# A gate product in seven block products instead of eight, in three units of a two-layer convolution and SwiGLU kernel

## The chip, the cores and the metric

The kernel runs on one core of one Trainium2 chip. The metric is the device time of one execution in microseconds, the median of several runs. The engines of the core are named as in the profile: PE (TensorE matmul), PEld (its weight loads), DVE (VectorE), ACT (ScalarE), POOL (GpSimd) and SP (SyncE, which here only issues DMAs).

## The reference

Two layers, each with a long convolution (A) and a SwiGLU feed-forward part (B), on 2048 tokens of 512 features in bf16. The feed-forward part has 1792 hidden features.

```python
def _B_ref(x, w_gate, w_up, w_down):
    g = _silu(x @ w_gate)
    u = x @ w_up
    return (g * u) @ w_down

x = A_q
x = x + _A_ref(_layernorm(x), A_k, A_v, A_shift_k, A_ssm_k, A_ssm_D)
x = x + _B_ref(_layernorm(x), B_w_gate, B_w_up, B_w_down)
x = x + _A_ref(_layernorm(x), A_k, A_v, A_shift_k, A_ssm_k, A_ssm_D)
x = x + _B_ref(_layernorm(x), B_w_gate, B_w_up, B_w_down)
return x
```

A multiplies its normalised input by a convolution of k and v over the whole sequence, which doesn't depend on x. The change touches only B.

## The kernel before

The sequence is cut into four chunks of 512 tokens, and each chunk into two halves of 256. A unit (l, c, h) is the feed-forward part of layer l for half h of chunk c, so there are 16 units. The last four are those of chunk 3: (0,3,0), (0,3,1), (1,3,0) and (1,3,1). Between a unit of layer 0 and the unit of layer 1 of the same half stand the down product's adds, two layer norms (bn_stats and bn_aggr on DVE, the power for rstd on POOL, L939) with the multiplication by the convolution's result between them, and transposing DMAs on SP, which turn z into zT, the operand of the next gate and up products. While one half goes through that chain, PE works on the other half.

A unit's 14 tiles of 128 hidden features come in groups of 4, 4, 4 and 2 (`GROUPS`). For each group `ffn` computes a gate half and an up half and multiplies them. Group 0 of the first three of the last units is done row-wise (`by_rows`). In the others, feature tiles are the stationary operand and 256 tokens the moving one: for each pair of feature tiles 8 matmuls of 256 columns into one PSUM buffer (ring `pf`, 4 buffers), then one ACT evacuation of 512 elements, a silu for the gate (L1321) and a copy for the up half (L1325). The product of the two is a DVE instruction (L1330).

Two parts are already computed with seven block products instead of eight. `seven` (L1130) does it for the down product in the units that `STRASSEN` names, with sums of weights made once (`weight_sums`) and sums of the activations (tile `cb`, L1139 to L1143), and `add_seven` adds the results. `up_seven` (L1210) does it for the up product in the groups that `UP7` names, groups 1 and 2 of the last four units. It views a group's operands as 2 x 2 blocks: contraction halves by odd and even feature tiles for the weights, contraction halves by the two token rows for zT. `up_sums` makes five sums of weight blocks once for a group (L1196, kept in ring `s8`), `z_sums` five sums of token blocks once for a unit (three instructions, L1204 to L1208). The seven products are then matmuls of 128 columns, 28 for a group (7 products, 2 pairs of tiles, 2 contraction blocks), into four PSUM buffers. ACT copies these to the tile m7 (L1236: three of 512 elements and one of 256), and four DVE instructions add and subtract them into the up tile (L1240 to L1245).

The program is a list of operations, each with an engine, what it reads and what it writes. `ORDER` is a table with one entry for each operation in the sequence in which the code creates them: the entry is the operation's place in the order of issue. Every engine takes its operations in the order of these places. Buffers of a ring are handed out in that order too, so an operation may also wait until a buffer comes free. `mode` answers "A" where its last argument is true and "D" where it is not, because `SUPER` is empty.

Of the kernel before, what the change touches and what calls it, by code (L numbers as in the profile page):

```python
# [9 lines left out]
P = 128  # L10
# [23 lines left out]
UP7 = {(0,3,0): (1, 2), (0,3,1): (1, 2), (1,3,0): (1, 2), (1,3,1): (1, 2)}  # L34
# [99 lines left out]
]  # L134
R = 4
BN_SLOTS = 6
# [228 lines left out]
def kernel(  # L365
# [14 lines left out]
    nc = tc.nc  # L380
# [7 lines left out]
    W = HP * P  # L388
# [1284 lines left out]
```

## Time and profile before

| | us |
|---|---|
| median of three runs | 337.94 (337.67 to 338.55) |
| the profiled execution, whole | 337.59 |
| its span, first to last instruction | 335.6 |

The span is what the views of the profile show; 2.0 us of the profiled execution lie around it. In a row that groups instructions stand: the line, the engine, the operation, what it writes and reads, the shapes and the count, then busy us and mean ns of one, then the engine's idle time before them and what ended it. A row of the chain has its start, its length, the engine and line. A row of the timeline has start, length, engine and line; instructions that follow each other on one line are merged (x4). Instructions of one engine overlap a little, so the step from one start to the next tells more of the rate than the length of one.

### The profile page before, as it was taken

To read this page: it belongs to the slowest core of one execution; us is meant where nothing else is said; L and a number is where in the kernel's file an instruction comes from. 1 tells how busy PE (TensorE), PEld (TensorE's weight loads), DVE (VectorE), ACT (ScalarE), POOL (GpSimd) and SP (SyncE) were. 2 spreads that over 40 slices of the span, in tenths; PEclk is the share of its full clock that TensorE was granted. 3 is DMA by queue.
4 is the path that set the end of the run, shared out by engine and by line. 5 is a ranking of instruction groups with operands and counts; after the bars stand their busy time and mean duration, and the time that the engine had idled before them with its cause. 6 is when DMAs were issued, how large, how long until landed. Compare 5 with 4: busy or idle time off the path is not lost.

```text
span 335.6 us, 6388 instructions
## 1 busy us (share of the span) xinstructions
PE 331.0 (99%) x2342; PEld 212.1 (63%) x2342; DVE 314.1 (94%) x601; ACT 267.1 (80%) x532; POOL 39.7 (12%) x54
## 2 busy tenths in 40 slices
PE   9999999999999999999999999999999999999996
PEld 7666864745445564654544564674747887978994
DVE  8899999999999999999999999999988789999495
ACT  7889999999988675799899765967787647867473
POOL 4000110032020010311101101151000000000000
PEclk9999999999999999999999999999999999999999
DMA  7999503367744488930744586727323210202201
GB/s 289 323 297 364 74 16 80 63 117 151 157 94 84 92 164 167 197 72 5 152 80 89 115 165 154 130 57 143 79 47 80 58 38 1 64 20 51 60 2 63
DMA packets 77449, 37.37 MB, mean 111 GB/s; under 512 B 67685, under 2 KB 73706, under 8 KB 77418
## 3 DMA queue, kind: packets, MB, share of 16 engines
q1 hardware_dynamic: 75632, 30.61, 39.0%
q0 software_dynamic: 1632, 6.29, 10.6%
q8 instruction: 18, 0.29, 0.4%
q14 instruction: 13, 0.11, 0.1%
q10 hardware_dynamic: 154, 0.07, 0.1%
HBM read 12.33 MB, written 2.10 MB: 43 GB/s over the span
## 4 chain that ended last, share of the span: by engine, by line
PE 94%; DVE 2%; DMA 1%; ACT 1%; POOL 0%; issue 0%; DVEq 0%; POOLq 0%
PE pf L437 51%; PE pd L1350 17%; PE ps L1160 10%; PE ps L437 7%; PE pf L1234 4%; PE ps L585 2%; DMA zT<-z 1%; PE wm L1639 1%; PE ps L918 1%; PE pt L604 1%; POOL rstd L939 0%; ACT kc L731 0%; DVE bst L953 0%; DVE t L783 0%; ACT sg L1260 0%
## 5 line engine op out<-in xcount | busy, mean ns | idle before, releaser
L437 PEld LDWEIGHTS <-zT 128*128 128x128 bf16 x496 | 48.2, 98 | 54.7 <-DMA zT<-z 0.5
L437 PE MATMUL pf<-wg_sb,zT 128*128 128x512 bf16 x248 | 61.5, 379 | 0.0
L437 PE MATMUL pf<-wu_sb,zT 128*128 128x512 bf16 x248 | 61.0, 379 | 0.0
L437 PE MATMUL pf<-zT,wg_sb 128*128 128x256 bf16 x400 | 50.4, 273 | 0.0
L437 PEld LDWEIGHTS <-wg_sb 128*128 128x128 bf16 x400 | 38.7, 98 | 7.6 <-issue 0.3
L1260 ACT ACTIVATE sg<-pf 128x512 bf16<-128x512 f32 x62 | 36.7, 607 | 8.2 <-PE pf L437 7.6
L1261 ACT CAST hr<-pf 128x512 bf16<-128x512 f32 x62 | 36.0, 592 | 8.3 <-PE pf L437 6.4
L1321 ACT ACTIVATE sg<-pf 128x512 bf16<-128x512 f32 x50 | 30.0, 610 | 14.9 <-PE pf L437 12.0
L779 DVE TENSOR_TENSOR t<-X,G 128x4096 bf16<-128x4096 bf16 x18 | 40.9, 2282 | 0.0
L1350 PE MATMUL pd<-wd_sb,sg 128*128 128x512 bf16 x160 | 38.6, 379 | 0.0
L939 POOL TENSOR_TENSOR rstd<-mv,nhalf 128x2 f32<-128x2 f32 x23 | 20.6, 900 | 138.6 <-DVE mv L954 138.6
L437 PE MATMUL pf<-zT,wu_sb 128*128 128x256 bf16 x272 | 34.4, 273 | 0.0
L953 DVE BATCH_NORM_STATS2 bst<-xc 128x6 f32<-128x512 bf16 x46 | 29.9, 683 | 0.4
L437 PEld LDWEIGHTS <-wu_sb 128*128 128x128 bf16 x272 | 26.6, 98 | 5.2
L1350 PEld LDWEIGHTS <-sg 128*128 128x128 bf16 x160 | 15.6, 98 | 17.8 <-DMA sg<-hr 0.3
L1350 PE MATMUL pd<-wd_sb,ht 128*128 128x512 bf16 (+1 forms) x110 | 25.5, 367 | 0.0
L1160 PEld LDWEIGHTS <-cb 128*128 128x128 bf16 x230 | 22.2, 98 | 4.5 <-DVE cb L1139 0.5
L1325 ACT CAST ht<-pf 128x512 bf16<-128x512 f32 x34 | 19.9, 598 | 3.5 <-PE pf L437 3.4
L546 ACT ACTIVATE X<-ps 128x512 bf16<-128x512 f32 x32 | 19.1, 610 | 3.5 <-PE ps L437 1.8
L1172 ACT CAST mt<-ps 128x512 bf16<-128x512 f32 (+1 forms) x28 | 14.5, 539 | 7.8 <-PE ps L1160 7.4
L1236 ACT CAST m<-pf 128x512 bf16<-128x512 f32 (+1 forms) x32 | 16.0, 541 | 3.6 <-PE pf L1234 3.3
L1330 DVE TENSOR_TENSOR ht<-ht,sg 128x1024 bf16<-128x1024 bf16 (+1 forms) x33 | 17.8, 554 | 1.1 <-ACT sg L1321 0.6
(157 smaller groups left out, 598.2 us busy)
## 6 DMA issues: line engine op xcount, KB each, us to landing
Z<-t POOLq DMA_DIRECT2D x6, 1024.0 KB, 8.3
hn<-in_A_ssm_k_dram SPq DMA_DIRECT2D x4, 512.0 KB, 4.9
vt<-in_A_v_dram SPq DMA_DIRECT2D x4, 512.0 KB, 5.3
xc<-in_A_q_dram SPq DMA_DIRECT2D x4, 512.0 KB, 6.1
out_dram<-xc SPq DMA_DIRECT2D x15, 128.0 KB, 1.9
wg_sb<-in_B_w_gate_dram SPq DMA_DIRECT2D x1, 1792.0 KB
wu_sb<-in_B_w_up_dram SPq DMA_DIRECT2D x1, 1792.0 KB, 7.8
wd_sb<-in_B_w_down_dram SPq DMA_DIRECT2D x1, 1280.0 KB, 12.0
```

The source lines that it names most:

```text
L437: nc.tensor.matmul(o, lhsT=lhsT, rhs=rhs, start=(n == 0), stop=(n == len(terms) - 1))
L546: add("ACT", act(D), lambda: nc.scalar.activation(out=view(), in_=ps.t[:], func=ACT.Copy, scale=scale), r=[ps], w=[(buf, keys)], conv=conv)
L779: dve(8 * D, lambda t=t, part=part: nc.vector.tensor_mul(out=t.t[:], in0=x.t[:, :, part:part + 1, :].to_broadcast((P, R, 2, D)), in1=g.t[: ...
L939: add("POOL", cost, lambda: nc.gpsimd.tensor_tensor(out=rstd.t[:], in0=var(), in1=nhalf.t[:].to_broadcast((P, n)), op=ALU.pow), r=reads + ...
L953: add("DVE", 0.6, lambda st=st, i=i: nc.vector.bn_stats(out=st.t[:, 0:6], in_=xs[c].t[:, i, :]), r=[(xs[c], (i,))], w=[st])
L1160: nc.tensor.matmul(bank.t[:, half_ * C:(half_ + 1) * C], lhsT=lhsT(i), rhs=rhs(i), start=(first and i == 0 and half_ == 0), stop=(last and ...
L1260: add("ACT", act(D), lambda ps=ps, dst=dst, o=o, which=which: nc.scalar.activation(out=rows(dst, o), in_=ps.t[:], func=ACT.Silu) if which ...
L1261: out=rows(dst, o), in_=ps.t[:], func=ACT.Silu) if which == "g" else nc.scalar.copy(out=rows(dst, o), in_=ps.t[:]),
L1321: add("ACT", act(D), lambda ps=ps, o=o, sg=sg: nc.scalar.activation(out=sg.t[:, o:o + 2, :], in_=ps.t[:], func=ACT.Silu), r=[ps], w=[(sg, ...
L1325: add("ACT", act(D), lambda ps=ps, o=o, ht=ht: nc.scalar.copy(out=ht.t[:, o:o + 2, :], in_=ps.t[:]), r=[ps], w=[(ht, (o // 2,))], due=(uni ...
L1330: dve(n * W, lambda sg=sg, ht=ht: nc.vector.tensor_mul(out=ht.t[:], in0=ht.t[:], in1=sg.t[:]), [sg], [ht], due=(unit, k / pairs, 0.0, "h"))
L1350: nc.tensor.matmul((pds[o] if not cs.start else pds[HP]).t[:, cs], lhsT=ht.tiles(q, o), rhs=wt["d"].t[:, ft, cs], start=(ft == std0 and no ...
```

## The change

The gate half of group 1 is computed with seven block products too, in units (0,3,0), (0,3,1) and (1,3,0). In each of them two standard products (16 matmuls of 256 columns) and their two silu evacuations from PSUM go. In their place come four operations on PE with 28 matmuls of 128 columns, four ACT copies to a tile m7, four DVE instructions that put the block sums together in the gate tile, and one ACT silu over the whole gate tile (1024 elements, in SBUF, in place), which waits for the last of the four. Five sums of gate weight blocks are made once, in another buffer of ring `s8`, and kept until the last of the three units has used them. The sums of token blocks are the ones that the up product uses. `up_sums` and `up_seven` take the weight's name; the calls of `up_sums` and `z_sums` move from `up_seven` to the place before the group's products in the list of operations.

`ORDER` is replaced as a whole: 1881 entries instead of 1849 (3 x 9 operations more, and 5 weight sums). Units keep their sequence. Of the table only the line with the places of the five gate weight sums is shown: they are operations 1462 to 1466, counted from 0, and stand as 1373, 1374, 1408, 1321, 1358.

```diff
-UP7 = {(0,3,0): (1, 2), (0,3,1): (1, 2), (1,3,0): (1, 2), (1,3,1): (1, 2)}
+UP7 = {(0,3,0): (1, 2), (0,3,1): (1, 2), (1,3,0): (1, 2), (1,3,1): (1, 2), "any": (1, 2)}
+GATE7 = {(0,3,0): (1,), (0,3,1): (1,), (1,3,0): (1,), "any": (1, 2)}
...
 ORDER = [
...
+    1518, 1535, 1533, 1546, 1550, 1373, 1374, 1408, 1321, 1358, 1417, 1406, 1390, 1062, 962, 1367, 972, 1369, 1407, 1410, 1411, 1412, 1428,
...
-    def up_sums(gi, kw):
+    def up_sums(which, gi, kw):
...
-    def up_seven(unit, zT, ht, fts, gi, at):
+    def up_seven(unit, zT, ht, fts, gi, at, which="u", before=()):
...
-        if gi not in wsum:
-            up_sums(gi, kw)
-        if unit not in zsum:
-            z_sums(unit, zT, kw)
-        w7, z7 = wsum[gi], zsum[unit]
+        w7, z7 = wsum[which, gi], zsum[unit]
...
-                seven_up = gi in UP7.get(unit, ())
+                kw = dict(due=(unit, k / pairs, 0.0, "h"))
+                sevens_at = {}
+                for which, table in (("g", GATE7), ("u", UP7)):
+                    s7 = sevens_at[which] = mode(which, unit + (gi,), gi in table.get(unit, ())) if c == 3 and gi in table.get("any", ()) else "D"
+                    if s7 in "AB":
+                        if (which, gi) not in wsum:
+                            up_sums(which, gi, kw)
+                        if unit not in zsum:
+                            z_sums(unit, zT, kw)
                 for o in range(0, n, 2):
-                    for which in ("g",) if seven_up else ("g", "u"):
+                    for which in "gu":
+                        if sevens_at[which] == "A":
+                            continue
...
-                if seven_up:
-                    up_seven(unit, zT, ht, fts, gi, k / pairs)
+                for which, dst in (("g", sg), ("u", ht)):
+                    if sevens_at[which] == "D":
+                        continue
+                    plan.cond = ((which,) + unit + (gi,), "A") if sevens_at[which] == "B" else None
+                    dst.steps = (W, P)
+                    up_seven(unit, zT, dst, fts, gi, k / pairs, which)
+                    if which == "g":
+                        add("ACT", 1.1, lambda sg=sg: nc.scalar.activation(out=sg.t[:], in_=sg.t[:], func=ACT.Silu), w=[sg],
+                            due=(unit, k / pairs, 1.0, "a"))
+                    plan.cond = None
```

More of the change, by code (lines that the diff above doesn't have):

```diff
@@ L33 @@
 STRASSEN={(0,2,1):4,(1,2,0):4,(1,2,1):4,(0,3,0):4,(0,3,1):4,(1,3,0):4,(1,3,1):2}
-UP7 = {(0,3,0): (1, 2), (0,3,1): (1, 2), (1,3,0): (1, 2), (1,3,1): (1, 2)}
+UP7 = {(0,3,0): (1, 2), (0,3,1): (1, 2), (1,3,0): (1, 2), (1,3,1): (1, 2), "any": (1, 2)}
+GATE7 = {(0,3,0): (1,), (0,3,1): (1,), (1,3,0): (1,), "any": (1, 2)}
+MODE0 = lambda g: int(g[4] in (UP7 if g[0] == "u" else GATE7).get(g[1:4], ()))
 I_RING = lambda k: "pf" if k == 3 else "pc"
@@ L1186 @@
     wsum, zsum = {}, {}
-    def up_sums(gi, kw):
+    def up_sums(which, gi, kw):
         fts = range(sum(GROUPS[:gi]), sum(GROUPS[:gi + 1]))
         m = len(fts) // 2
-        t = wsum[gi] = new("s8", "wu", [P, 5, KD // 2, m, P], parts=5)
-        part = lambda k, f: wt["u"].t[:].rearrange("p k (t f) -> p k t f", f=P)[:, 2 * k:2 * k + 2, fts[0] + f:fts[-1] + 1:2]
+        t = wsum[which, gi] = new("s8", "w" + which, [P, 5, KD // 2, m, P], parts=5)
+        part = lambda k, f: wt[which].t[:].rearrange("p k (t f) -> p k t f", f=P)[:, 2 * k:2 * k + 2, fts[0] + f:fts[-1] + 1:2]
         for n, (a, b, op) in enumerate((((0, 0), (1, 1), ALU.add), ((0, 1), (1, 1), ALU.add), ((0, 0), (1, 0), ALU.add),
@@ L1196, in up_sums @@
             dve(2 * m * P, lambda n=n, a=a, b=b, op=op: nc.vector.tensor_tensor(out=t.t[:, n], in0=part(*a), in1=part(*b), op=op),
-                [wt["u"]], [(t, (n,))], **kw)
+                [wt[which]], [(t, (n,))], **kw)
     def z_sums(unit, zT, kw):
@@ L1208, in z_sums @@
         dve(K2 * P, lambda: nc.vector.tensor_add(out=t.t[:, 0], in0=at(0, [[W, K2]]), in1=at(K2 * W + P, [[W, K2]])), [zT], [(t, (0,))], **kw)
-    def up_seven(unit, zT, ht, fts, gi, at):
+    def up_seven(unit, zT, ht, fts, gi, at, which="u", before=()):
         m, K2 = len(fts) // 2, KD // 2
         kw = dict(due=(unit, at, 0.0, "h"))
-        if gi not in wsum:
-            up_sums(gi, kw)
-        if unit not in zsum:
-            z_sums(unit, zT, kw)
-        w7, z7 = wsum[gi], zsum[unit]
+        w7, z7 = wsum[which, gi], zsum[unit]
         mt = new("s8", "m7", [P, 4, 2, m, P], parts=4)
-        raw = lambda k, f, i: (lambda kk: wt["u"].t[:, k * K2 + kk, (fts[0] + 2 * i + f) * P:(fts[0] + 2 * i + f + 1) * P])
+        raw = lambda k, f, i: (lambda kk: wt[which].t[:, k * K2 + kk, (fts[0] + 2 * i + f) * P:(fts[0] + 2 * i + f + 1) * P])
         summed = lambda n, i: (lambda kk: w7.t[:, n, kk, i])
@@ L1224, in up_seven @@
         for n, (rd, terms) in enumerate((
-                ([wt["u"], (z7, (2,))], ((lambda i: raw(0, 0, i), both(3)), (lambda i: raw(1, 1, i), both(4)))),
+                ([wt[which], (z7, (2,))], ((lambda i: raw(0, 0, i), both(3)), (lambda i: raw(1, 1, i), both(4)))),
                 ([w7, zT], ((lambda i: summed(2, i), tok(1, 1)), (lambda i: summed(1, i), tok(0, 0)))),
@@ L1308, in ffn @@
                 ht.tiles, ht.steps = (lambda q, o, ht=ht: ht.t[:, q, o * P:(o + 1) * P]), (W, P)
-                seven_up = gi in UP7.get(unit, ())
+                kw = dict(due=(unit, k / pairs, 0.0, "h"))
[7 more added lines that the diff above has]
+                            z_sums(unit, zT, kw)
                 for o in range(0, n, 2):
-                    for which in ("g",) if seven_up else ("g", "u"):
+                    for which in "gu":
+                        if sevens_at[which] == "A":
+                            continue
+                        plan.cond = ((which,) + unit + (gi,), "D") if sevens_at[which] == "B" else None
                         ps = new("pf", "pf", [P, D], F32)
@@ L1326, in ffn @@
                                 r=[ps], w=[(ht, (o // 2,))], due=(unit, k / pairs, 1.5, "a"))
+                        plan.cond = None
                     k += 1
-                if seven_up:
-                    up_seven(unit, zT, ht, fts, gi, k / pairs)
+                for which, dst in (("g", sg), ("u", ht)):
[7 more added lines that the diff above has]
+                            due=(unit, k / pairs, 1.0, "a"))
+                    plan.cond = None
                 dve(n * W, lambda sg=sg, ht=ht: nc.vector.tensor_mul(out=ht.t[:], in0=ht.t[:], in1=sg.t[:]), [sg], [ht],
```

151 rows, old and new, of the table ORDER are left out of this document.

## The prediction, made before the changed kernel was run

> **What bounds the kernel now.** I read the page's busy times first, and then asked whether the busy engine is also the one that sets the end.
>
> ```profile
> span 335.6 us, 6388 instructions
> PE 331.0 (99%) x2342; PEld 212.1 (63%) x2342; DVE 314.1 (94%) x601; ACT 267.1 (80%) x532; POOL 39.7 (12%) x54
> PE 94%; DVE 2%; DMA 1%; ACT 1%; POOL 0%; issue 0%; DVEq 0%; POOLq 0%
> ```
>
> PE is busy 331.0 of 335.6 us, and the chain of work that ended last (third line) runs through PE for 94% of the span. So a column taken from PE shortens the kernel, as long as nothing makes PE wait. DVE stands second with 314.1 us, so the next question is where DVE has room. I cut the program into stretches: the middle, the way into the last four units, and one stretch for about each of those.
>
> ```profile
> 88.00:216.00 128.00, 127.98 (x694) 67.53 (x691) 126.97 (x183) 103.26 (x209) 14.88 (x15) 1.00 0.58 117
> 216.00:256.00 40.00, 39.53 (x264) 25.19 (x262) 37.58 (x89) 30.20 (x56) 7.71 (x8) 1.00 0.43 83
> 256.00:281.00 25.00, 25.00 (x246) 20.90 (x244) 20.70 (x59) 15.37 (x31) 0.38 (x1) 1.00 0.21 43
> 281.00:298.00 17.00, 17.00 (x170) 14.01 (x168) 16.14 (x45) 12.72 (x24) 1.40 (x2) 1.00 0.18 41
> 298.00:315.00 17.00, 17.00 (x169) 14.01 (x167) 15.34 (x42) 9.38 (x19) 1.39 (x2) 1.00 0.23 56
> 315.00:333.00 18.00, 17.38 (x180) 15.04 (x177) 13.31 (x33) 13.00 (x27) 0.00 (x0) 1.00 0.06 18
> ```
>
> The columns after the length are busy us of PE, weight loads, DVE, ACT and POOL, then granted clock, DMA share and GB/s. From 88 to 216 us PE and DVE are both full: DVE idles 1.03 us in 128. In the last units PE stays full and DVE has room: 2.42, 4.30, 0.86, 1.66 and 4.69 us in the five later rows. ACT has at least 4 us in each. The clock is 1.00 throughout. Last, what does PE wait for? These are the rows of its weight loads after the first 40 us (us in total, times, longest), and the two of the matmuls themselves.
>
> ```profile
> PEld L437 <- DMA zT<-z: 0.5, 1, 0.5
> PEld L1160 <- DVE ht L1330: 0.5, 1, 0.5
> PEld L1160 <- DVE cb L1139: 0.5, 1, 0.5
> PEld L1350 <- DMA sg<-hr: 0.3, 1, 0.3
> PEld L1160 <- DVE cb L1143: 0.2, 1, 0.2
> PEld L1350 <- DVE ht L1330: 0.2, 1, 0.2
> PE ps L1160 <- DVE ht L1330: 0.3, 1, 0.3
> PE ps L1160 <- DVE cb L1139: 0.2, 1, 0.2
> ```
>
> All waits of the weight loads come to 2.2 us, 1.4 of it on DVE, and only 0.5 shows through as matmuls that waited. That is all that a better order can win after the start. The new table keeps every other operation on its engine and the units in their sequence; SP's transposes and POOL's operations are shuffled with the rest, none moves to another queue.
>
> **The products themselves.** In each of three units the standard gate product of one group, 16 matmuls of 256 columns, gives way to 28 of 128 columns (seven products, two pairs of feature tiles, two contraction blocks). The chain shows both shapes in unbroken runs:
>
> ```profile
> 305.90 3.49 PE pf L437 x32
> 320.79 1.56 PE pf L1234 x28
> ```
>
> 3.49 / 32 = 0.109 us for one of 256 columns, 1.56 / 28 = 0.0557 us for one of 128. So 16 x 0.109 = 1.745 us become 1.56: 0.185 us less in a unit, and 0.56 us in three. The second row is just such a group in this kernel, so I take it as it stands. The columns alone (512 fewer of 4096 in a unit) would save 12.5%, of which 10.6% is left.
>
> A rule speaks against this. The rows that group all 128-column products by operands are these:
>
> ```profile
> L1234 PE MATMUL pf<-zs,wu 128*128 128x128 bf16 x96 | 7.5, 219 | 0.0
> L1234 PE MATMUL pf<-zs,wu_sb 128*128 128x128 bf16 x64 | 4.9, 219 | 0.0
> L1234 PE MATMUL pf<-zT,wu 128*128 128x128 bf16 x64 | 4.7, 219 | 0.0
> ```
>
> They are busy 17.1 us for 224, which is 0.076 us each, because the modelled tail of each short run is counted along. The Trainium skill (TensorE: Matmul & The Clock Gate, Back-to-back issue gap) says that in a real stream of weight load and matmul pairs a matmul of 128 columns takes some 81 ns, not the isolated 56. By it a unit's 28 would take 2.27 us, and the edit would lose 0.5 us a unit. The run of 28 in 1.56 us disagrees with that rule, and it decides for the sum.
>
> **What DVE and ACT get.** The steps:
>
> ```profile
> 268.26 0.42 DVE L1242 TENSOR_TENSOR m<-m 128x512 bf16<-128x512 bf16 x1
> 268.60 0.42 DVE L1245 TENSOR_TENSOR ht<-m 128x512 bf16<-128x512 bf16 x1
> L1236 ACT CAST m<-pf 128x512 bf16<-128x512 f32 x24 | 13.5, 594 | 2.7 <-PE pf L1234 2.4
> L1236 ACT CAST m<-pf 128x256 bf16<-128x256 f32 x8 | 3.1, 385 | 0.9 <-PE pf L1234 0.9
> L1321 ACT ACTIVATE sg<-pf 128x512 bf16<-128x512 f32 x50 | 30.0, 610 | 14.9 <-PE pf L437 12.0 <-DMA sg<-hr 2.2 <-ACT z L1004 0.3
> L614 ACT COPY hs<-pt 128x1024 bf16<-128x1024 bf16 x2 | 2.0, 1020 | 0.0
> L718 ACT COPY hr<-hn 128x512 bf16<-128x512 bf16 x8 | 5.4, 685 | 0.0
> L614 ACT COPY hs<-pt 128x512 bf16<-128x512 bf16 x2 | 1.1, 576 | 0.0
> ```
>
> A sum of 512 elements steps DVE by 268.60 - 268.26 = 0.34 us. Five weight sums once are 1.7 us, four block sums in each of three units are 12 x 0.34 = 4.1 us: 5.8 us on DVE. The token sums existed before and are only created earlier. ACT loses two silus from PSUM (1.22 us) and gains three evacuations of 512, one of 256 and a silu over 1024 elements in SBUF, which the trace doesn't have: a copy of 1024 from PSUM took 1.02, and SBUF instead of PSUM cost 0.685 - 0.576 = 0.11 at 512, so 1.13 as an estimate from these rows. That is 1.78 + 0.385 + 1.13 - 1.22 = 2.1 us a unit, 6.2 in all, under ACT's room of at least 4 us a row.
>
> DVE's 5.8 us meet 2.42 + 4.30 + 0.86 + 1.66 = 9.24 us of room from 216 to 315. They cost nothing if the order spreads them so; without that cover each us in front of a down product is a us of PE. The new table's five entries for the weight sums are 1373, 1374, 1408, 1321 and 1358, which is the approach to unit (0,3,0) and not the full stretch before 216. Nothing is added there, so I count no cost for them, and at worst their 1.7 us.
>
> **The added wait.** The one silu now waits for the last block sum on DVE, and behind it on ACT stand evacuations that free PE's four PSUM buffers. In unit (1,3,0) the silu's place is 1751, DVE's product with the up half 1752, and PE's first matmuls that read the product come next in PE's queue. What covers the silu's 1.13 us is only how far ACT and DVE run ahead of PE there, so this edge is thin; it hangs on the same DVE queue as the next one, and I price them together.
>
> **The order's other thin edge.** The first product of the last unit (1,3,1) needs zT, which comes from the down product of (0,3,1) through adds, two layer norms and transposing DMAs. In the kernel before:
>
> ```profile
> 296.65 0.93 PE L1160 MATMUL ps<-wsa,cb 128*128 128x256 bf16 x7
> 297.42 0.61 PE L1234 MATMUL pf<-zs,wu_sb 128*128 128x128 bf16 x8
> 307.74 2.50 SPq L1061 DMA_TRANSPOSE zT<-z  x2
> zT<-z SPq DMA_TRANSPOSE x4, 2.4
> 313.82 1.04 PE L437 MATMUL pf<-zT,wg_sb 128*128 128x256 bf16 x8
> ```
>
> PE is done with (0,3,1) at 297.42 and reads the new zT at 313.82, 16.4 us later. The second transpose is issued 1.25 us (half of 2.50) after 307.74 and lands 2.4 us on, at 311.4: a chain of 14.0 us with 2.4 to spare. In the old table 7 matmuls of (1,3,0)'s down product stand behind that first read (entries above 1742), in the new one 25 (entries above 1764). So 18 x 0.109 = 1.96 us of work no longer lies in between, and 0.19 of the gate product is gone: 16.4 - 2.15 = 14.25 us for a chain of 14.0. The spare time falls from 2.4 to about 0.2 us. On DVE that chain now has (1,3,0)'s four gate sums among its entries, 1.36 us, while other sums have moved behind. A wait here costs between nothing (the sums fill gaps in which rstd and DMAs run) and 1.36 - 0.2 = 1.2 us; I take nothing: from the last add of (0,3,1) to the second z the old table has six sums and two products of 1024 elements beside the norms, the new one eight sums and one product, which is about the same work.
>
> **The sum.** PE -0.56, waits unchanged: 337.59 (the profiled execution, 335.6 of span and 2.0 around it) becomes 337.03. The median of the three runs, 337.94, is 0.35 above it, so what should be measured beside it is 337.94 - 0.56 = **337.4**. A measurement of this kernel can tell about 0.3%, 1.01 us, from no change: from 336.93 to 338.95 counts as the same.
>
> **The rivals.**
>
> 1. *The new order also removes waits.* The 1.4 us on DVE and 0.5 on zT go, of which 0.5 at least was PE's own. It would come to -0.56 - 0.5 to -0.56 - 1.4, that is 336.9 to 336.0; I put it at 336.4. For it: the waits are few and in places that the new table shuffles. Against: DVE is full up to 216, the waits on cb and ht stand at its end, and the new table takes no DVE work out ahead of it.
>
> 2. *The last zT comes late.* Its place is the first read by (1,3,1), decided by whether the chain exceeds 14.25 us; from 1.57 us of wait on the result is slower by over 0.3%. Price: 1.2 us of gate sums, and a rstd on POOL that DVE holds up.
>
> ```profile
> L939 POOL TENSOR_TENSOR rstd<-mv,nhalf x23: 686/710/2572, 29.9 to 306.0; 128x2 f32<-128x2 f32 x23
> ```
>
> Its median is 710 ns and its longest 2572, 1.86 us more, which gives 337.94 - 0.56 + 1.2 + 1.86 = 340.4; with 1.6 us of wait it would be 339.0. Against it: from 281 to 315 the four spans on POOL took 1.40 + 1.39 us, 0.70 each, beside a DVE that was busy all along. The Trainium skill (SBUF — State Buffer, Who interferes with whom) says that a DVE instruction with two SBUF inputs holds off a GpSimd instruction that reads SBUF for its whole length; the longest rstd agrees, and every added sum is of that kind.
>
> 3. *Products of 128 columns don't hold their pace.* At the grouped rows' 0.076 us 28 take 2.13 us, 0.39 more than before in each unit: 337.94 + 1.2 = 339.1. By the page named above it would be 339.5. The unbroken run of 28 speaks against it.
>
> **How the numbers follow.** Forecast 0.46, rival 1 0.31, rival 2 0.18, rival 3 0.05. Rival 1 lies below 336.93: faster 0.31. Same is 0.46. Rivals 2 and 3 give slower 0.23. Forecast and rival 1 hold 77%, and the forecast's own range is 336.9 to 338.6 (its wait of up to 1.2 us). For 8 in 10 the range takes in rival 1 to 336.2 and the lower part of rivals 2 and 3 to 339.4.
>
> **What would show it.** Right: 28 added products at 0.056 us, PE's busy time lower by about half a us, DVE up by some 6 us with its busy share in 256 to 315 above nine tenths, and no new row on zT or ht among PE's waits in the last units. A wait of over 1.5 us at the first read of (1,3,1), or one on ht of (1,3,0), means rival 2. A run of 28 that takes over 2 us means rival 3. If the old waits on cb and ht are gone and no others came, it is rival 1. I am wrong in kind if PE's waits lie before 216, where the change adds no work and only the order differs.

## The result and the profile after

The changed kernel took 340.64 us (median of five runs, 340.31 to 341.93), the kernel before 337.67 beside it (337.13 to 338.55): a ratio of 1.0092, 95% interval 1.0078 to 1.0107. The forecast was 337.4 with a range up to 339.4, so the kernel is 3.2 us slower than forecast and outside the range. The profiled execution took 340.31 us. Its page, span and busy times first, then the chain that ended last by engine and by line:

```profile
span 338.5 us, 6471 instructions
PE 331.5 (98%) x2378; PEld 210.6 (62%) x2378; DVE 318.2 (94%) x618; ACT 272.9 (81%) x541; POOL 45.1 (13%) x54
PE 38%; DVE 33%; ACT 11%; DMA 7%; issue 6%; POOL 3%; SPq 0%; POOLq 0%; DVEq 0%; ACTq 0%
PE pf L441 16%; PE ps L1164 8%; DMA Z<-t 6%; PE pf L1234 5%; PE ps L441 4%; DVE bst L957 3%; POOL rstd L943 3%; DVE t L783 3%; DVE m L671 3%; DVE t L787 3%; DVE hr L1267 3%; PE ps L589 2%; ACT z L1008 2%; DVE n L1057 2%; ACT hr L1261 1%
```

The busy times hardly tell the two kernels apart: PE has half a microsecond more, probably because the modelled tail of the matmul ahead of a gap counts as busy and there are more gaps (at 84 us a matmul starts 0.86 us later than the usual step, and 0.70 of it shows as idle). The chain tells them apart. It ran through PE for 94% of the span and now does for 38%; DVE, ACT, the transfer Z<-t and the rstd on POOL have come into it. The same stretches as before, and one ahead of them (columns as in the prediction):

```profile
40.00:88.00 48.00, 47.30 (x276) 26.83 (x275) 46.12 (x71) 47.89 (x95) 10.06 (x8) 1.00 0.46 81
88.00:216.00 128.00, 126.89 (x680) 65.79 (x678) 124.79 (x178) 100.49 (x202) 16.67 (x15) 1.00 0.60 117
216.00:256.00 40.00, 39.30 (x266) 25.28 (x265) 38.13 (x89) 30.64 (x59) 8.55 (x7) 1.00 0.41 77
256.00:281.00 25.00, 25.00 (x233) 19.07 (x232) 24.03 (x71) 17.57 (x33) 0.69 (x1) 1.00 0.36 70
281.00:298.00 17.00, 17.00 (x183) 14.15 (x182) 15.21 (x40) 14.05 (x27) 1.41 (x2) 1.00 0.12 25
298.00:315.00 17.00, 17.00 (x183) 14.14 (x182) 16.58 (x47) 12.82 (x25) 1.38 (x2) 1.00 0.25 56
```

From 256 to 315 us, where the change is, PE is full as before: 25.00, 17.00 and 17.00. From 88 to 216, where nothing was added, PE idles 1.11 us instead of 0.02 and DVE 3.21 instead of 1.03. To see where the time goes I added up the columns that PE has worked off in both kernels and compared the times at which they reach the same amount. The changed kernel is level until 76 us, 0.6 us late at 88, 1.1 at 108, 1.7 at 132, 2.2 at 148, 2.3 at 212, 2.6 at 232, 3.0 at 240, 3.5 at 244, and between 3.3 and 3.6 from there to 256. Its whole work on PE is 0.55 us less, and 3.5 less 0.55 is about the 2.9 us by which the span grew. So it looks as if the products do what was forecast, and the new order loses 3.5 us ahead of the stretch that the products are in. PE's own waits, the largest of the rows that grew (us in total, times, longest):

```profile
PEld L1370 <- DMA sg<-hr: 3.0, 5, 0.8
PE pd L1370 <- DMA sg<-hr: 1.1, 3, 0.6
PE ps L441 <- DVE Z L677: 0.7, 1, 0.7
PEld L1164 <- DVE cb L1143: 1.1, 3, 0.6
```

Some names in the rows that follow: X, G, t, Z and m belong to the convolution, where a transfer on POOL's queue adds t into Z and m is made from Z. A layer norm's mean and variance are mv (DVE, from bst) or nm and ve (ACT, by way of jk); rstd and nmr are the scale and the shift made from them. In the row-wise parts hr becomes the product of the gate and the up half, and sg its transpose by a transfer on SP.

The first place is at 84 us. The changed kernel's chain there, start and length:

```profile
69.29 0.30 ACT ve L988
69.76 2.57 POOL rstd L943
72.33 8.59 DMA Z<-t
80.95 1.23 DVE m L671
```

On POOL's queue the new table puts an rstd (of ve) ahead of the first Z<-t, the 1 MB transfer whose end m<-Z waits for. It used to stand behind. The timeline of POOL and DVE, the kernel before first and the changed one second:

```profile
69.81 1.39 POOL L787 DMA_DIRECT2D Z<-t  x1 [5.59 <-DVE t L783]
71.42 0.85 POOL L939 TENSOR_TENSOR rstd<-ve,nhalf 128x2 f32<-128x2 f32 x1 [0.22 <-ACT ve L984]
```

```profile
69.55 2.28 DVE L783 TENSOR_TENSOR t<-X,G 128x4096 bf16<-128x4096 bf16 x1
69.73 2.65 POOL L943 TENSOR_TENSOR rstd<-ve,nhalf 128x2 f32<-128x2 f32 x1 [5.51 <-DVE t L787]
72.33 1.37 POOL L791 DMA_DIRECT2D Z<-t  x1
80.95 1.23 DVE L671 TENSOR_TENSOR m<-Z 128x2048 bf16<-128x2048 bf16 x1 [1.47 <-DMA Z<-t]
```

The rstd took 2.65 us beside t<-X,G, the transfer was issued 2.5 us later than before, and DVE idled 1.47 us ahead of m<-Z.

The theory after this comparison, "order": the new table adds waits ahead of 246 us that cost 3.5 us, and the products pay 0.55. Its rival, "units": the added sums, the silu or their buffers cost the time in the last units, and what the early stretches show is an accident. A third, "buffers": the gate's weight sums take up room and shift the transfers in any order.

### The profile page after: what moved, and what is told of

Read it like the earlier page. It is cut to its first block, busy times and chain, and to the rows that moved or that the text cites. A ratio compares the mean times of both kernels' runs of the same rounds, so it can differ in the third digit from the quotient of the medians.

```text
span 338.5 us, 6471 instructions
## 1 busy us (share of the span) xinstructions
PE 331.5 (98%) x2378; PEld 210.6 (62%) x2378; DVE 318.2 (94%) x618; ACT 272.9 (81%) x541; POOL 45.1 (13%) x54
## 4 chain that ended last, share of the span: by engine, by line
PE 38%; DVE 33%; ACT 11%; DMA 7%; issue 6%; POOL 3%; SPq 0%; POOLq 0%; DVEq 0%; ACTq 0%
PE pf L441 16%; PE ps L1164 8%; DMA Z<-t 6%; PE pf L1234 5%; PE ps L441 4%; DVE bst L957 3%; POOL rstd L943 3%; DVE t L783 3%; DVE m L671 3%; DVE t L787 3%; DVE hr L1267 3%; PE ps L589 2%; ACT z L1008 2%; DVE n L1057 2%; ACT hr L1261 1%
## 5 line engine op out<-in xcount | busy, mean ns | idle before, releaser
L441 PE MATMUL pf<-zT,wg_sb 128*128 128x256 bf16 x352 | 43.6, 273 | 0.1
L1260 ACT ACTIVATE sg<-pf 128x512 bf16<-128x512 f32 x62 | 36.9, 604 | 7.0 <-PE pf L441 5.3
L943 POOL TENSOR_TENSOR rstd<-mv,nhalf 128x2 f32<-128x2 f32 x23 | 23.7, 1034 | 135.9 <-DVE mv L958 126.4
L441 PEld LDWEIGHTS <-wg_sb 128*128 128x128 bf16 x352 | 34.3, 98 | 6.9 <-issue 0.3
L1332 ACT ACTIVATE sg<-pf 128x512 bf16<-128x512 f32 x44 | 26.3, 613 | 10.7 <-PE pf L441 6.6
L1236 ACT CAST m<-pf 128x512 bf16<-128x512 f32 (+1 forms) x44 | 20.4, 556 | 0.6 <-PE pf L1234 0.5
```

The costliest lines, as they stand in the source:

```text
L441: nc.tensor.matmul(o, lhsT=lhsT, rhs=rhs, start=(n == 0), stop=(n == len(terms) - 1))
L943: add("POOL", cost, lambda: nc.gpsimd.tensor_tensor(out=rstd.t[:], in0=var(), in1=nhalf.t[:].to_broadcast((P, n)), op=ALU.pow), r=reads + ...
L1236: add("ACT", act(len(terms) * m * P), lambda n=n, ps=ps, terms=terms: nc.scalar.copy(out=mt.t[:, n, 0:len(terms)], in_=ps.t[:, 0:len(terms)]),
L1260: add("ACT", act(D), lambda ps=ps, dst=dst, o=o, which=which: nc.scalar.activation(out=rows(dst, o), in_=ps.t[:], func=ACT.Silu) if which ...
L1332: add("ACT", act(D), lambda ps=ps, o=o, sg=sg: nc.scalar.activation(out=sg.t[:, o:o + 2, :], in_=ps.t[:], func=ACT.Silu), r=[ps], w=[(sg, ...
```

## The experiments

Each ratio is to the kernel before on the same chip, with its 95% interval. In the moves the numbers are places in `ORDER`.

**1 to 4: the order and the products apart.** Nothing of the code is changed, only which table orders which stretch.

```diff
 1: code of after;  places of before up to 242 us, of after behind
 2: code of before; places of after throughout
 3: code of before; places of after up to 246 us, of before behind
 4: code of before; places of after up to 130 us, of before behind
```

1: 

> The code of the kernel after, with the 28 block products, their weight sums and the new silu; the instructions stand in the order of the kernel before up to about 242 us, and in the order of the kernel after behind that. The theory 'order' (the waits that the new table adds ahead of 246 us cost 3.5 us, the products pay 0.55) expects 337.1, that is 0.994 to 0.999 of the kernel before, and PE gaps of after at 84, 109, 131, 134 and 147 us gone. The rival 'units' (the sums, the new silu or their buffers in the last units cost the time) expects 340 to 341. A third, 'buffers' (the added weight sums hold buffers and shift the transfers in any order), expects 338 to 340.

2: 

> The code of the kernel before, with its 16 products for each gate, in the order of the kernel after from start to end. 'Order' expects the products' 0.55 us on top of after: 341.2, ratio 1.010. 'Units' expects no cost without the products: 337.7. 'Buffers' expects something between, 338 to 339.5.

3: 

> The code of the kernel before; the order of after up to about 246 us, that of before behind it. 'Order' expects the whole 3.5 us to stand at 246 already: 341.2, ratio 1.010, as with the new order to the end. 'Units' expects 337.7. If the late part of the new table costs something too, this run is faster than the one with the new order throughout by that much.

4: 

> The code of the kernel before; the order of after up to about 130 us, that of before behind it. 'Order' expects the lag that stands at 108 to 132 us, 1.1 to 1.8 us: 338.8 to 339.5, ratio 1.0035 to 1.0055. 'Units' expects 337.7. If the queue makes up for what was lost early, 'order' is wrong in that its lags add up, and this run is near 337.7 as well.

Measured: 1 at 0.9986 (0.9974 to 0.9998), 337.33 us; 2 at 1.0113 (1.0091 to 1.0135); 3 at 1.0109 (1.0092 to 1.0126); 4 at 1.0085 (1.0067 to 1.0103). "Order" holds on both sides: the products without the new order are 0.5 us faster than before, and the new order without the products is as slow as the change or slower (0.7 us by the ratios, whose intervals overlap). "Units" and "buffers" fall. The fourth cost 2.9 us, more than expected: in its trace, as in that of after, PE is about 1.7 us late at 132, but then 2.6 at 156 and 3.0 from 224 on, in stretches that have the old order. (Some matmuls are missing from this trace, so these three are estimates.) So what is lost early is not made up for later. Whether the further loss comes of being late or of the passage from one order to the other, this run can't tell.

**5: the rstd ahead of the first Z<-t, in the kernel before.**

```diff
-rstd<-ve 451, Z<-t 435
+rstd<-ve 435, Z<-t 436
```

> The kernel before with one instruction moved: on the GpSimd queue the rstd of ve stands ahead of the first Z<-t transfer instead of behind it (the place that it has in after). 'Held rstd' (rstd runs until the row of two-input VectorE instructions beside it has ended, and holds the transfer behind it) expects rstd at about 69.8 us with some 2.6 us instead of 0.85, the transfer issued at 72.3 instead of 69.8 and landed near 80.5 instead of 77.9, VectorE idle by 1 to 1.5 us ahead of m<-Z, a PE gap of 0.6 to 0.9 us near 84 us, and 338.4 to 338.7 us in all (ratio 1.002 to 1.003). The rival 'transfer' (the first Z<-t is late in after because of the loads beside it, not because of rstd) expects rstd under 1 us, the transfer no more than 0.9 us later, no gap near 84, and 337.8.

1.0029 (1.0018 to 1.0040), 338.91 us. POOL, DVE and PE in its timeline:

```profile
71.49 0.84 POOL L939 TENSOR_TENSOR rstd<-ve,nhalf 128x2 f32<-128x2 f32 x1 [7.18 <-ACT ve L984]
72.29 1.39 POOL L787 DMA_DIRECT2D Z<-t  x1
81.28 1.23 DVE L667 TENSOR_TENSOR m<-Z 128x2048 bf16<-128x2048 bf16 x1 [1.50 <-DMA Z<-t]
83.45 1.04 PE L1350 MATMUL pd<-wd_sb,sg 128*128 128x512 bf16 x4 [1.37 <-DMA sg<-hr]
```

The place alone costs 1.0 us: the transfer goes at 72.29, DVE idles 1.50 and PE loses some 1.4 us, through hr and its transposes. But the mechanism was not the one that I expected here. The rstd took 0.84, not 2.6; POOL sat idle for 7.18 us until ACT had made ve, with a finished t<-t,t behind it. In both kernels the transfer stands behind an rstd that isn't done before 72.3: here for want of its input, in after because it ran long.

**6: the load of vt early, in the kernel before.** In after this 512 KB load is issued at 128 us among the transposes that PE waits for, before it was issued at 159.

```diff
-vt load 887
+vt load 715
```

> The kernel before with one transfer moved: the 512 KB load of vt for the last chunk is issued between the transposes and the output writes at about 127.5 us, as in after, instead of at 159 us. 'Queue' (this load, in front of the output writes and the transposes on SP's queue and beside the second Z<-t, makes them late) expects the sg<-hr transposes behind it 0.6 to 1.5 us later, the second Z<-t to land later than its 8.4 us after the issue, a PE gap of 0.5 to 0.9 us near 131 us, and 338.3 to 338.7 (ratio 1.0015 to 1.003). The rival 'inherited' (the gap of after at 131 us is only the lag of its first Z<-t, carried on) expects 337.8 and no new gap.

1.0071 (1.0044 to 1.0099), 339.89 us: 2.0 us more than before, over the price that "queue" had put on it. SP's queue and the two waits:

```profile
127.20 1.31 SPq L509 DMA_DIRECT2D vt<-in_A_v_dram  x1
132.84 0.34 SPq L513 DMA_DIRECT2D xc<-in_A_q_dram  x1
133.46 1.90 PE L1350 MATMUL pd<-wd_sb,sg 128*128 128x512 bf16 x8 [0.66 <-DMA sg<-hr]
136.43 1.29 DVE L953 BATCH_NORM_STATS2 bst<-xc 128x6 f32<-128x512 bf16 x2 [1.56 <-DMA xc<-in_A_q_dram]
```

The load of xc was issued at 130.61 before and at 132.84 here, two transposes follow it, and DVE's statistics wait for it. The second Z<-t was not slowed (8.5 us to landing instead of 8.4), so that part of the expectation is wrong.

**7 and 8: the same two places undone in the kernel after.**

```diff
 7: -rstd<-ve 427, Z<-t 433
    +rstd<-ve 433, Z<-t 432
 8: -vt load 719
    +vt load 882
```

7: 

> The kernel after with the rstd of ve put behind the first Z<-t on the GpSimd queue, as in before. 'Held rstd' expects the gap of 0.86 us at 84 us gone or under 0.3, the transfer issued at 69.8, and 0.5 to 0.9 us less than after (ratio to before 1.0065 to 1.0077, after being at 1.0092); if the later waits hang on that lag too, more than that, down to 1.004. 'Transfer' expects no change: 1.009.

8: 

> The kernel after with the 512 KB load of vt for the last chunk put back to about 156 us, behind the second and third Z<-t. 'Queue' expects the gaps at 131 and 134 us (0.73 and 0.14) to shrink to 0.3 or less in sum, the second Z<-t to land 8.4 instead of 10.1 us after its issue, and 0.6 us less than after: ratio to before 1.0075. 'Inherited' expects the gap at 131 us as it is, ratio 1.009.

7 stands at 1.0060 (1.0038 to 1.0082), 8 at 1.0088 (1.0070 to 1.0105). With rstd behind, the gap at 84 us is gone, and at 212 us PE is some 1.1 us behind the kernel before instead of 2.3 (again an estimate from a trace with some matmuls missing). Putting the load back gained nothing in the whole, though PE's idle time at 131 us shrank from 0.57 to 0.27. These rows count the second Z<-t from issue to landing, from 118 to 132 us in before, after and the eighth run:

```profile
Z<-t POOLq DMA_DIRECT2D x1, 1024.0 KB, 8.4
```

```profile
Z<-t POOLq DMA_DIRECT2D x1, 1024.0 KB, 10.1
```

```profile
Z<-t POOLq DMA_DIRECT2D x1, 1024.0 KB, 9.8
```

It stays at 9.8 without the load, and t<-X,G still waits 1.58 us for it. The load is harmful where it was put alone, but it isn't what makes this transfer late in after.

**9: the long rstd at 218 us, in the kernel of run 1.** One bst<-xc and its mv<-bst move between the last mv and t<-X,G, so that rstd starts beside an instruction with one input.

```diff
-bst<-xc 1145, mv<-bst 1157
+bst<-xc 1163, mv<-bst 1164
```

> The kernel of the first experiment (old order to 242 us, block products of after) with two VectorE instructions moved: one bst<-xc (0.69 us, one input) and its mv<-bst, which stand some 0.8 us ahead of the last mv<-bst before t<-X,G at 218.68, go between that mv and t<-X,G. The rstd that took 2.57 us there beside t<-X,G then starts beside bst. 'Held' (a GpSimd instruction that starts during a two-input VectorE instruction runs until the row of them ends) expects that rstd at 0.7 to 0.9 us, VectorE's idle 0.58 us ahead of nmr gone, the two PE gaps near 222 and 224 us (0.39 and 0.42) at 0.3 or less in sum, and 336.6 to 337.0 (ratio to before 0.9965 to 0.998). The rival 'slow in itself' (this rstd waits for its input or is long for a reason on GpSimd) expects 2.57 us again and 0.9985.

0.9988 (0.9977 to 0.9998): no gain over run 1.

```profile
212.73 0.73 DVE L1013 TENSOR_SCALAR n<-xc,nm,rstd 128x512 bf16<-128x512 bf16 x2 [0.51 <-POOL rstd L943]
217.69 0.69 POOL L943 TENSOR_TENSOR rstd<-mv,nhalf 128x2 f32<-128x2 f32 x1 [5.00 <-DVE mv L958]
218.68 2.38 POOL L943 TENSOR_TENSOR rstd<-ve,nhalf 128x2 f32<-128x2 f32 x1 [0.30 <-ACT ve L988]
221.31 0.61 PE L1164 MATMUL ps<-wd_sb,cb 128*128 128x256 bf16 x4 [0.33 <-DVE cb L1143]
```

The rstd took 0.69 instead of 2.57, and the next one, which now began beside t<-X,G, took 2.38 instead of 0.68: the length goes with the DVE instruction in whose course it begins. The time did not follow. The bst had filled another wait of DVE, which now shows at 212.73 (0.51), and cb came to PE no earlier.

**10: ve earlier, in the kernel after.** ACT's two jk and ve go ahead of its two z.

```diff
-jk 424, jk 425, ve 426; z 418, z 420
+jk 418, jk 419, ve 420; z 421, z 423
```

> The kernel after with ScalarE's three instructions that make ve (two jk, one ve) put ahead of the two z instead of behind them: ve is ready near 68.3 us instead of 69.6, while VectorE runs ht, t<-t,t, t<-t,t and t<-X,G, all with two inputs, without a break from 66.9 to 71.8. 'Held' expects no gain from the earlier ve: rstd starts near 68.4, runs for 3.5 to 4 us, the first Z<-t is issued at 72.3 as in after, the PE gap of 0.86 us at 84 stays, ratio 1.009 (up to 1.010, since z is 1.3 us later). The rival 'queued' (the transfer is late because rstd waits for ve, as it was in the run with rstd moved ahead in the kernel before) expects rstd to end by 69.2, the transfer at 69.8, no gap at 84, and 1.006.

1.0120 (1.0100 to 1.0139), but for another reason than "held" gave. Its rstd, the transfer and two new waits of PE:

```profile
68.61 0.72 POOL L943 TENSOR_TENSOR rstd<-ve,nhalf 128x2 f32<-128x2 f32 x1 [4.10 <-ACT ve L988]
70.51 1.38 POOL L791 DMA_DIRECT2D Z<-t  x1 [1.19 <-issue]
73.03 1.90 PE L441 MATMUL pf<-wu_sb,zT 128*128 128x512 bf16 x8 [1.14 <-DMA zT<-z]
247.40 1.04 PE L441 MATMUL pf<-wu_sb,zT 128*128 128x512 bf16 x4 [1.53 <-DMA zT<-z]
```

The rstd began inside t<-t,t, an instruction with two inputs and another such behind it, and took 0.72. So it isn't held until a row of them ends. The gap at 84 us went, as "queued" said; z, which had to make way, made zT late and cost 1.1 us of idle time at 73. By this trace that isn't what makes the kernel slower than after: from 148 to 236 us PE is as late as there (2.0 us against 2.2 at 148, 2.5 in both at 236), and what is lost on top is the 1.53 us at 247, where the transposes zT<-z took up to 5.0 us; run 17 comes back to them. Runs 7 and 10 together: at 70 us the first Z<-t is late in after because an rstd that starts 0.2 us into t<-X,G stands ahead of it, and either an earlier ve or the other place on the queue cures that.

**11 and 12: which stretch costs what.**

```diff
 11: code of after; places of before up to 208 us, of after behind
 12: code of after; places of before up to 130 us, of after behind
```

11: 

> The code of after with the order of before up to about 208 us and that of after behind it. The first experiment went over at 242 us and stands at 0.9986. 'Each stretch its own' (the new order of 208 to 242 us costs its 1.0 to 1.3 us by itself) expects 338.3 to 338.7, ratio 1.0015 to 1.0030. 'Carried on' (those waits come of VectorE being late from 84 and 131 us) expects 337.3, ratio 0.9985.

12: 

> The code of after with the order of before up to about 130 us and that of after behind it; the mirror of the run that took the new order to 130 us and cost 2.9 us. 'Each stretch its own' expects the waits of after behind 140 us (0.3 at 147, 1.3 at 214 to 245) again: 338.3 to 339.0, ratio 1.0015 to 1.0040. 'Carried on' expects 337.3, ratio 0.9985.

11 at 1.0034 (1.0019 to 1.0048), 12 at 1.0042 (1.0027 to 1.0057). With run 1 at 0.9986 and after at 1.0092 the loss divides so: 1.0092 - 1.0042 = 0.50%, 1.7 us, for the new order up to 130 us; 0.08%, 0.3 us and within the noise, from 130 to 208; 0.48%, 1.6 us, from 208 to 242. "Each stretch its own" holds for the last stretch, which costs its 1.6 us with the old order ahead of it. But these shares hold for this way round only: with the new order in front, in runs 3 and 4, the part up to 130 us costs 0.85% and the part from there to 246 only 0.24%. So the stretches don't simply add up. In the last of them DVE waits twice for an rstd, and PE for cb (run 11):

```profile
237.43 2.16 POOL L943 TENSOR_TENSOR rstd<-mv,nhalf 128x2 f32<-128x2 f32 x2 [4.40 <-DVE mv L958]
233.06 0.73 DVE L1013 TENSOR_SCALAR n<-xc,mv,rstd 128x512 bf16<-128x512 bf16 x2 [0.61 <-POOL rstd L943]
238.96 0.16 DVE L997 SCALAR_TENSOR_TENSOR nmr<-mv,rstd 128x2 f32<-128x2 f32 x1 [0.38 <-POOL rstd L943]
223.45 0.61 PE L1164 MATMUL ps<-wd_sb,cb 128*128 128x256 bf16 x4 [0.49 <-DVE cb L1143]
```

**13 to 16: those places undone.** The moves of 13, 14 and 16 are on DVE; 15 has those of 7, 13 and 14 in the kernel after.

```diff
 13, run 11 with: m<-Z 1275 -> 1287, nmr 1284 -> 1288 (behind three cb<-sg)
 14, run 11 with: nmr 1182 -> 1187 (behind two cb<-sg); cb<-sg 1195, 1197 -> 1194, 1195; t<-t,t 1194 -> 1196
 16, run 1 with:  nmr 1177 -> 1181 (behind two cb<-sg)
```

13: 

> The kernel with the old order to 208 us (1.0034 of before), with one move on VectorE near 237 us: the first m<-Z and the nmr behind it go behind the three cb<-sg, as in the order of before. 'VectorE's order' (the new table lets rstd start beside m<-Z, holds nmr and puts the cb that PE waits for behind both) expects rstd at 237.4 at 0.7 us instead of 1.50, the idle 0.38 us ahead of nmr gone, the PE gaps at 238 and 241 us (0.33 and 0.28) gone, 338.1 to 338.3, ratio 1.0012 to 1.0020. 'Full anyway' (VectorE has too much to do between 208 and 242 us in the new table, so that a wait taken away here comes back within the next few us) expects 1.0034 as it was.

14: 

> The same kernel with a move near 221 us instead: nmr goes behind the two cb<-sg that follow it, which fill the 0.58 us for which VectorE waits for the held rstd (2.57 us beside t<-X,G), and the next two cb<-sg go ahead of t<-t,t (1.22 us). 'VectorE's order' expects the PE gaps at 220.7 and 222.7 us (0.24 and 0.65) at 0.3 or less in sum and 338.1 to 338.4, ratio 1.0012 to 1.0022. 'Full anyway' expects 1.0034.

15: 

> The kernel after from start to end in its new order, with three mends: rstd behind the first Z<-t as in the seventh run (1.0060), and the moves near 221 and 237 us of the two runs beside this one. If these are the places where the new order loses, the three are worth 1.1 + 0.5 + 0.5 us and the kernel stands at 338.4 to 338.7, ratio 1.0015 to 1.0030; what is left then are the gaps at 131 to 148 us. 'Full anyway' expects 1.0060 or more.

16: 

> The kernel of the first experiment (block products of after, old order to 242 us, 0.9986) with nmr behind the two cb<-sg that follow it at 221 us, so that these fill VectorE's 0.58 us of waiting for the held rstd. 'VectorE's order' expects the PE gap of 0.39 us near 222 gone and that of 0.42 near 224 at 0.2 or less: 336.7 to 337.0, ratio 0.9965 to 0.9978. 'Full anyway' expects 0.9986.

13 stands at 1.0022 (1.0009 to 1.0035), some 0.4 us less than run 11 and nearer to its first expectation, but the two intervals overlap, so the gain isn't clear of the noise. Its trace shows what the move did: the gap at 238 us is gone and DVE's idle ahead of nmr too, the gap at 241 shrinks from 0.28 to 0.16, and the two rstd still take 2.38 us together. 14 stands at 1.0041 (1.0028 to 1.0054), no gain and perhaps a loss, by an error of mine:

```profile
222.26 0.43 DVE L1143 TENSOR_TENSOR cb<-sg 128x512 bf16<-128x512 bf16 x1 [0.74 <-DMA sg<-hr]
224.55 0.28 PE L1164 MATMUL ps<-wst,ht 128*128 128x256 bf16 x1 [0.63 <-DVE ht L1350]
```

The cb that I moved ahead of t<-t,t had to wait for its own transpose, and ht, which PE needs too, came later. 15 stands at 1.0057 (1.0042 to 1.0072): with 14 in it, it gains nothing over run 7, so that the sum of the mended places isn't shown. 16 does what was expected, 0.9969 (0.9958 to 0.9980), 336.80 us: two cb fill the 0.58 us for which DVE waited for the held rstd. The difference to run 1, 0.17%, is just clear of the noise of the two. The rstd is as long as ever, with nobody waiting for it:

```profile
218.03 2.57 POOL L943 TENSOR_TENSOR rstd<-mv,nhalf 128x2 f32<-128x2 f32 x1 [5.00 <-DVE mv L958]
219.97 0.42 DVE L1145 TENSOR_TENSOR cb<-sg 128x512 bf16<-128x512 bf16 x1
220.65 0.16 DVE L997 SCALAR_TENSOR_TENSOR nmr<-mv,rstd 128x2 f32<-128x2 f32 x1
221.16 0.60 PE L1164 MATMUL ps<-wd_sb,cb 128*128 128x256 bf16 x4
```

Neither nmr nor this read of cb has an idle time in front of it any more. It is the fastest kernel of the study: 1.0 us less than before, of which by the medians the products have 0.5 and one moved instruction 0.5. The wait that it takes away is no loss of the new order: the kernel before has it too, with an rstd of 2.57 us at 217.57, DVE's 0.58 us behind it, and these two waits of PE, which the prediction listed among its old ones:

```profile
221.07 0.61 PE L1160 MATMUL ps<-wd_sb,cb 128*128 128x256 bf16 x4 [0.22 <-DVE cb L1139]
222.81 0.39 PE L1160 MATMUL ps<-wst,ht 128*128 128x256 bf16 x2 [0.26 <-DVE ht L1330]
```

**17: runs 7 and 8 together, in the kernel after.**

> The kernel after with two mends: rstd behind the first Z<-t (alone 1.0060) and the 512 KB load of vt for the last chunk put back to about 156 us (alone 1.0088, no gain). 'Two causes' (once the first Z<-t is in time, the load is what makes the transposes at 131 to 134 us late, as it did when it was put there in the kernel before) expects the PE gaps of 0.24 and 0.52 us near 130 and 133 us at 0.3 or less in sum, and 339.2 to 339.5, ratio 1.0040 to 1.0048. 'Another cause' (the rest of the new order between 84 and 130 us makes the second Z<-t and those transposes late) expects the gaps as they are and 1.0060.

1.0087 (1.0064 to 1.0110): no gain over run 8, and none over after, though the interval reaches down to that of run 7. Its profiled execution agrees with neither theory: at 212 us PE is some 1.0 us behind the kernel before, better than the 2.3 of after, but 1.8 us are lost at 244 us, where the transposes zT<-z took up to 5.1 us. Run 7's profiled execution, at 341.34 us the longest of its six, has the same thing in its chain:

```profile
240.34 0.81 ACT z L1008
241.18 4.93 DMA zT<-z
246.16 1.04 PE pf L441 x4
```

The longer of the two transposes at this place took 2.6 us in before and 3.1 in after. The other traces, one execution each, fall into groups: 2.6 to 2.8 us in all seven kernels that have the old order here (before, 1, 4, 5, 6, 9, 16), 2.8 and 3.0 in runs 13 and 15, which have the move at 237 us, 3.1 to 4.0 in the other kernels with the new order (after, 2, 3, 8, 11, 12, 14), and 4.9 to 5.1 in 7, 10 and 17. These three are the ones that have the first Z<-t in time and the new order as it was from 208 us on. So curing the first Z<-t came with a new loss of 1.5 to 1.8 us at 244 to 247 us in each of their profiled executions. Why, and why the second Z<-t takes 9.8 us in the new order, is not settled.

## Why the prediction was wrong

- *PE bounds the kernel.* Right for the kernel before, and its chain shows it. In the kernel after PE is still busy for 98%, but the chain is on PE for only 38%: it runs through what PE waits for.
- *The products, -0.56 us.* Right. The 28 matmuls run as forecast, in this row of the changed kernel's chain, and run 1, which has the products and not the new waits, is 0.49 us under the kernel before (0.1 to 0.9 by the interval). The rival of slow products falls, and with it, for this stream, the 81 ns that the Trainium skill (TensorE: Matmul & The Clock Gate, Back-to-back issue gap) gives a matmul of 128 columns: here it is 56.

```profile
260.10 1.56 PE pf L1234 x28
```

- *DVE and ACT, nothing.* Right. DVE got 4.1 us (5.8 estimated), ACT 5.8 (6.2), and from 256 to 315 us, with DVE busy for 94.6% instead of 88%, PE didn't lose a hundredth.
- *The thin edges in the last units, nothing.* Right in the kernel after: no row of PE or its weight loads on zT or ht among its waits behind 256 us. Some of the variants (7, 8, 12, 13, 17) show 0.2 to 0.4 us of idle time at the first read of (1,3,1), within the 0 to 1.2 that the prediction gave it.
- *Waits unchanged.* This is the step that failed. The prediction looked at the new table as something that can only win, up to the 2.2 us of the old waits ("all that a better order can win"), and bounded what it can lose at the places only where operations were added. From 88 to 216 us PE and DVE were both full in the old order, 127.98 and 126.97 of 128: that is not a stretch in which the order is free, since the old one fits and another may not. Instead of "unchanged", the new one lost 3.5 us between 76 and 246, 2.3 of them by 212, where the change adds no work, and runs 2 and 3 lose as much without the products. The closing sentence named this case ("wrong in kind if PE's waits lie before 216"), but no rival had it, and it had no share in the chances.
- *Rival 1* was right that there were old waits to win: run 16 fills the one at 220 us and gains some 0.5 us. The new table as it was didn't win it; in after PE's weight loads wait for cb for longer than before (1.1 us in the row shown).
- *Rival 2* had a mechanism of the right kind at the wrong place: a rstd held by DVE, with its 1.86 us. The Trainium skill (SBUF — State Buffer, Who interferes with whom) was drawn on for the last zT; it applied at 70 us, where the new table put such a rstd ahead of the first Z<-t, and that could be read from the two tables and the row of 2572 ns. The runs agree with the rule that a two-input DVE instruction holds up a GpSimd instruction that reads SBUF (2.57 us beside t<-X,G, 0.69 beside bst<-xc in run 9).

Shown by experiments: that the order and not the products costs the time (1 to 3), that the stretch from 208 to 242 us costs 1.6 us by itself (1, 11), and that the rstd ahead of the first Z<-t makes it late (5, 7, 10), which cost 1.0 us in the kernel before and 1.1 in after (7; 15 agrees, 17 doesn't repeat the gain). Shown in the trace, but not clear of the noise in the time: the cb and nmr behind m<-Z near 237 us (13, 0.4 us). Only argued: the cb behind t<-t,t at 222 us. Open: what in the order makes the second Z<-t slow and the transposes at 130 to 148 us late, and the transposes at 244 us. More than half of the 3.5 us is so traced to no single place.

## What to carry to other kernels

A change that replaces the whole order of issue is two changes, and the second can cost or gain wherever two engines are full; read the two tables against each other at each transfer that a full engine waits for, above all what stands ahead of it on its queue. Measure the two apart (the new code in the old order, the old code in the new order): run 1 gave back the gain that the sum had right, and run 2 showed the loss alone. A wait that can't be shortened may be filled with work that is ready, which was worth about as much here as the products; a move that takes no account of when its inputs land (14), or opens another wait (9), is worth nothing.

## What the runs showed of the hardware

- An rstd of 2 x 128 elements takes some 0.7 us on POOL (0.69 beside bst<-xc, which has one input). Where it begins 0.2 us into t<-X,G (2.28 us) it takes 2.57 to 2.65, and ends 0.55 us after that instruction. Begun 0.2 us before the end of a t<-t,t, with the next one right behind, it took 0.72, and ended 0.55 us after the first (run 10). The same 0.55 us stands in all nineteen traces: of 224 rstd that took over 0.84 us, 215 end 0.53 to 0.59 us after the end of a DVE TENSOR_TENSOR, which reads two inputs, and in 204 of them it is the one in whose course the rstd began. The one at 97 us in after took 3.03: it began beside a z with one input, went on across three instructions with two inputs, and ended 0.55 us after the third. Why it wasn't released after the first isn't known. The other nine are all the rstd near 84 us that follows directly on another.
- A transfer whose data is ready waits behind whatever stands ahead of it on POOL's queue: 2.5 us behind an rstd that had no input yet (run 5).
- The longer of the two transposes zT<-z at 241 us took 2.8 to 5.1 us from issue to landing in the kernels that have the new order there, and 2.6 to 2.8 in those with the old one.
